# Copies out of PSUM moved from ScalarE to VectorE in an attention and expert kernel

## The chip, the cores and the metric

The kernel runs on one core of one Trainium2 chip. The metric is the device time of one execution in microseconds. Engines are named as in the profile: PE (TensorE), DVE (VectorE), ACT (ScalarE), POOL (GpSimd), SP (SyncE, which issues transfers here).

## What is computed

Local and global attention, and on its output a layer of experts of which each row takes at most one:

```python
scale = 1.0 / np.sqrt(D)                      # batch 8, heads 8, D = 64
s_g = scale * q_g @ concat(k_g, k_l).T        # 32 global queries see all 544 keys
out_g = softmax(s_g) @ concat(v_g, v_l)
s_ll = where(|i - j| <= 32, scale * q_l @ k_l.T, -1e9)   # 512 local queries: a band
a_l = softmax(concat(scale * q_l @ k_g.T, s_ll))         # and the 32 global keys
out_l = a_l @ concat(v_g, v_l)
x = concat(out_g, out_l) as rows              # 8 * 544 = 4352 rows of 512
do = x @ w_skip > 0
e = argmax(x @ w_gate); gate = softmax(x @ w_gate)[e]
out = x, plus for rows with do: gate * (relu(x @ w1[e]) @ w2[e])
```

All in fp32; the experts' products are made of split fp32 parts.

## The kernel before

The attention part goes over 32 pairs of heads (4 pairs in each of 8 batches). The loop at the end of the attention part takes one **unit** u for each pair and is a software pipeline of three: in unit u the pair `cur` (u) gets its scores and exponentials, `prev` (u - 1) its normalization and transposes, `old` (u - 2) its products with the values. Instructions stand on each engine in the order in which this code is written, so the loop's body is the schedule. A pair has 8 blocks of 64 queries, and a block sees 160 keys.

In the order of the body, a unit does this:

- `cur.scores(0)`: PE makes the scores of four blocks (L343); DVE adds the mask and takes the minimum (L355); ACT takes the exponential with its sum (L360).
- `prev.normal(1)`, `prev.scale(1)`: DVE sums and inverts (L385, L386), POOL multiplies (L390). In odd units `prev.normal_g` does the same for the global queries (L420 and L421 on DVE, L422 on POOL).
- `batch_rows(b, k)`: for an earlier batch b, PE turns 128 finished columns of `xT` into rows (L540 into `pr`), ACT copies them out of PSUM (L541) and SP sends them to `out`. With k = 0 come the logits of the batch on PE (L549), which ACT copies (L553), with k = 3 their transposes (L559), which DVE reduces (L560).
- `old.values(0)`, `values(1)`, `values_g`: PE multiplies the probabilities with the values into two PSUM tiles, `pvs[0]` for even blocks of queries and `pvs[1]` for odd ones (L474, L481, L493). ACT copies both into `xT` (L501, two instructions of 128x256). `prev.turn_g(0)`: a stream transpose on DVE (L458).
- `cur.normal(0)`, `cur.scale(0)`, `cur.scores(1)`: as above, for the other half of the pair.
- `old.gather_g(0)`, `gather_g(1)`: DVE adds up the global queries' part of the two tiles (L508, L506). `prev.turn_g(1)`: L458 again.
- `prev.turn(0)`, `turn(1)`: PE transposes the probabilities (L430); DVE copies the first half out of PSUM, ACT the second (L433).
- in odd units `prev.turn_pg`: PE transposes the global probabilities (L442, L443), copied by DVE and ACT (L448, L451). In even units `cur.scores_g`: PE scores of the global queries for two pairs (L405), their minimum on DVE (L409), their exponential on ACT (L414).
- from unit 4, for as long as there are weights of the first expert left: a cast on ACT and a subtraction on POOL (L181, L182), 16 in all.

`batch_rows` runs with k = (u - 6) mod 4 in units 6 to 25 for the batches 0 to 4, so odd k falls into odd units. Batch 3 has a fifth piece, the global rows (L523, in unit 21). The rows of batches 5 and 6 come later in the body, after `gather_g` (`LATE_ROWS`): (5,0) and (5,1) in unit 25, (5,2) in 26, (5,3) in 27, and all four of batch 6 in unit 29. In units 25 and 29 that is the unit in which `old` is the last pair of that batch. Batch 7 goes through `rows` (L523, L528) at the end.

The PSUM tiles of tag "t" (`pr`, `pst`, `psl`, `pl`, `pq`) share three buffers, those of tag "v" (`pv`) two; `xr`, the rows on their way out, has five buffers in SBUF. After the attention part the rows are gathered by expert with indirect transfers, and the experts follow (L827 to L930), PE busy nearly throughout.

Of the kernel before, what the change touches and what calls it, by code (L numbers as in the profile page):

```python
# [28 lines left out]
QB = 64  # L29
# [14 lines left out]
def kernel(  # L44
# [12 lines left out]
    nc = tc.nc  # L57
# [9 lines left out]
    def ps_t(name):  # L67
        return ps.tile([P, 512], F32, tag="t", name=name, bufs=3)
# [117 lines left out]
    with ExitStack() as actx:  # L186
# [130 lines left out]
        def head(h):  # L317
            return slice(h * D, (h + 1) * D)

        def pair(u):  # L320

            b, p = divmod(u, NP)
            q, k, vv = qs[u % NQ], ks[u % NQ], vw[u % NV]
# [129 lines left out]
            pvs = {}  # L453
# [33 lines left out]
            def values_g():  # L487
                for o in range(2):
                    for odd in range(2):
                        pvi = pvs[odd][:, 0:384].rearrange("d (j r) -> d j r", r=96)  # L490
                        for h in range(2):
                            s = head(h ^ odd)
                            nc.tensor.matmul(  # L493
                                pvi[head(h), :, o * SG:(o + 1) * SG], vg[s, p, o, head(h)],
                                pgTs[0][s, odd:NB:2, :], start=False, stop=o == 1,
                                skip_group_check=True,
                            )
                x4 = xT[b][:, p, :].rearrange("d (j a q) -> d a j q", a=2, q=QB)
                for odd in range(2):
                    pvi = pvs[odd][:, 0:384].rearrange("d (j r) -> d j r", r=96)  # L500
                    nc.scalar.copy(x4[:, odd], pvi[:, :, 0:QB])  # L501

            def gather_g(odd):
                pv, xg = pvs[odd], xTg[b // 4][:, p, b % 4, :]
                if odd:
                    nc.vector.tensor_add(xg, xg, pv[:, QB:96])  # L506
                else:
                    nc.vector.reduce_sum(  # L508
                        xg, pv[:, 0:384].rearrange("d (s r) -> d r s", r=96)[:, QB:96, :],
                        axis=AX.X,  # L510
                    )

            return SimpleNamespace(
                scores=scores, normal=normal, scale=scale, scores_g=scores_g,
                normal_g=normal_g, turn=turn, turn_pg=turn_pg, turn_g=turn_g,
                values=values, values_g=values_g, gather_g=gather_g,
            )

        def rows(src, lg, k, dsts, halves, xr):
            for c2 in halves:  # L520
                pr = ps_t("pr")
                for c in range(2):
                    nc.tensor.matmul(  # L523
                        pr[:, c * XW:(c + 1) * XW], src(2 * c2 + c), idw[:, 2 * c2 + c, :],
                        start=True, stop=True,
                    )
                pv = pr[:, 0:2 * XW].rearrange("p (c n) -> p c n", n=XW)
                nc.scalar.copy(  # L528
                    xr[:, c2 * 256:(c2 + 1) * 256].rearrange("p (c n) -> p c n", n=P),
                    pv[:, :, 0:P],  # L530
                )
                nc.vector.tensor_copy(lg[:, k, 2 * c2:2 * c2 + 2, :], pv[:, :, P:XW])
            if halves[-1] == 1:
                for part, r0, n in dsts:
                    nc.sync.dma_start(out[r0:r0 + n, :], xr[part:part + n, :])

        def rows_turn(src, xr, dsts):
            pr = ps_t("pr")
            for c in range(NC):
                nc.tensor.transpose(pr[:, c * P:(c + 1) * P], src(c), ident)  # L540
            nc.scalar.copy(xr, pr)  # L541
            for part, r0, n in dsts:
                nc.sync.dma_start(out[r0:r0 + n, :], xr[part:part + n, :])

        def logits(b):

            pl = ps_t("pl")
            for c in range(NC):
                nc.tensor.matmul(  # L549
                    pl[c * 32:(c + 1) * 32, :], w32[:, c, :], xT[b][:, c, :],  # L550
                    start=True, stop=True,
                )
            nc.scalar.copy(lT, pl)  # L553

        def logits_turn(lg):
            pq = ps_t("pq")
            for t in range(4):
                ts_ = slice(t * P, (t + 1) * P)
                nc.tensor.transpose(pq[:, ts_], lT[:, ts_], ident)  # L559
            stages.insert(0, lambda: nc.vector.reduce_sum(  # L560
                lg[:, 0:4],
                pq.rearrange("p (t c e) -> p t e c", t=4, c=NC)[:, :, 0:E + 1, :],
                axis=AX.X,
            ))
# [75 lines left out]
        lgb, lgs, lgw, xrs = {}, {}, {}, {}  # L640
        LK = 0

        def batch_rows(b, k, halves=(0, 1)):
            T = 5 if b % 4 == 3 else 4
            whole = b < B - 1
            bs = (b,) if b >= B - 2 else (b - b % 2, b - b % 2 + 1)
            t0 = 4 * (b - bs[0])
            if b not in lgs:
                if b == bs[0]:
                    lgw[b] = (  # L650
                        wk.tile([P, 9, E + 1], F32, name="lg2") if len(bs) > 1
                        else rt.tile([P, 5, E + 1], F32, name="lg", bufs=2)
                    )
                lgs[b] = lgw[bs[0]][:, t0:t0 + T]
                if T == 5:
                    lgb[b] = rt.tile([P, 5, NC, E + 1], F32, name="lgb", bufs=1)
            if halves[0] == 0:
                xrs[b, k] = sm.tile([P, DM], F32, name="xr", bufs=5)
            hf = b // 4

            def src(c):
                if k < 4:
                    return xT[b][:, c, k * P:(k + 1) * P]
                return xTg[hf][:, c, :, :].rearrange("d b q -> d (b q)")

            dsts = [(0, b * S + SG + k * P, P)]
            if k == 4:
                dsts = [(bb * 32, (4 * hf + bb) * S, 32) for bb in range(4)]
            if k < 4 and whole:
                rows_turn(src, xrs[b, k], dsts)  # L670
                if k == LK:
                    logits(b)
                if k == 3:
                    logits_turn(lgs[b])
            else:
                rows(src, lgb[b], k, dsts, halves, xrs[b, k])
            if k == T - 1 and halves[-1] == 1:
                if T == 5:
                    ts_ = slice(4 if whole else 0, 5)
                    stages.append(lambda: nc.vector.reduce_sum(  # L680
                        lgs[b][:, ts_], lgb[b][:, ts_].rearrange("p t c e -> p t e c"), axis=AX.X
                    ))
                if b != bs[-1]:
                    return
                T += t0
                steps, send = route(
                    bs, lgw[bs[0]][:, 0:T], T, nc.vector if b >= B - 2 else nc.gpsimd
                )
                stages.extend(steps)
                if b == B - 2:  # L690
                    stages.append(
                        lambda: nc.vector.tensor_scalar_max(base[:, 0:1], base[:, 0:1], float(GRP))
                    )
                stages.append(lambda: sends.extend([lambda t=t: send(t) for t in range(T)]))
# [5 lines left out]
        with tc.manual_schedule(engines=engines):  # L700
# [19 lines left out]
            for u in range(NU + 2):  # L720
# [14 lines left out]
                def late_rows():  # L735
                    for b, k in LATE_ROWS.get(u, ()):
                        batch_rows(b, k)
                    if u == NU - 1:
                        for k in range(5):
                            batch_rows(B - 1, k, (0,))  # L740
# [11 lines left out]
                if 0 <= bp < B - 3:  # L752
                    batch_rows(bp, kp)
                    if kp == 3 and bp % 4 == 3:
                        batch_rows(bp, 4)
# [328 lines left out]
```

## Time and profile before

| | us |
|---|---|
| three runs | 1484.32, 502.81, 506.65 |
| their median | 506.65 |
| the profiled execution | 501.2 |
| its span, first to last instruction | 499.4 |

| engine | busy us | share of the span | instructions |
|---|---|---|---|
| PE | 454.5 | 91% | 4962 |
| DVE | 300.0 | 60% | 1221 |
| ACT | 290.8 | 58% | 883 |
| POOL | 228.2 | 46% | 236 |

The attention part fills about the first 240 us of the span, the experts the rest. A timeline row gives start, duration, engine, line, operation, output<-input, shape and count; in brackets stands the idle time of that engine just before, and what ended it. A count over 1 means that several instructions of the kind are merged into one row. A row of a line's own view gives the shortest, median and longest duration in ns. A row of the waits gives the total in us, the number of waits and the longest.

### The profile page before, as it was taken

The numbers are of one execution on the slowest core, as the hardware profiler recorded it, in microseconds if no ns is written. First come the engines' busy times: TensorE is split into PE (matmuls) and PEld (weight loads), VectorE is DVE, ScalarE is ACT, GpSimd is POOL, SyncE is SP. The second block draws the span as 40 slices with busy tenths as digits, with TensorE's granted clock in tenths as the row PEclk, the third lists the DMA queues.
The fourth block names the chain that finished last, engine by engine and source line by source line (L and its number), as shares of the span: only waits on it lengthen the run. The fifth ranks groups of instructions, "written<-read, shape, count | busy, mean of one in ns | idle before, by whom it ended". The sixth has DMA issues, their size and how long they took to land. (4 is left out here: it accounts for less than half of the span.)

```text
span 499.4 us, 13645 instructions
## 1 busy us (share of the span) xinstructions
PE 454.5 (91%) x4962; PEld 367.2 (74%) x4962; DVE 300.0 (60%) x1221; ACT 290.8 (58%) x883; POOL 228.2 (46%) x236
## 2 busy tenths in 40 slices
PE   8898999999989998888699999999999999999991
PEld 3575676676666776566597979798978989788881
DVE  6886767877657867784344318783923848157210
ACT  5688999899877888765342208481713635245200
POOL 6556666668864667767345015142300431023200
PEclk9999999999999999999799999999999999999997
DMA  8989888888977798720446406975740849203100
GB/s 250 274 294 319 255 278 243 286 281 188 282 207 229 241 190 265 162 65 2 150 170 170 158 24 197 366 235 191 249 153 7 278 174 323 82 26 129 46 15 17
DMA packets 50545, 93.32 MB, mean 187 GB/s; under 512 B 15596, under 2 KB 19948, under 8 KB 50448
## 3 DMA queue, kind: packets, MB, share of 16 engines
q1 hardware_dynamic: 44624, 81.83, 52.5%
q0 software_dynamic: 5824, 10.25, 6.2%
q8 instruction: 55, 0.90, 0.8%
q14 instruction: 42, 0.34, 0.2%
HBM read 82.91 MB, written 14.67 MB: 195 GB/s over the span
## 5 line engine op out<-in xcount | busy, mean ns | idle before, releaser
L360 ACT ACTIVATE prob<-prob,nmx 128x160 f32<-128x160 f32 x256 | 106.4, 418 | 16.4 <-DVE nmx L355 14.9
L390 POOL TENSOR_TENSOR prob<-prob,inv 128x640 f32<-128x640 f32 x64 | 80.1, 1257 | 32.1 <-ACT prob L360 15.4
L853 ACT ACTIVATE hh<-ph 128x256 fp32r<-128x256 f32 x72 | 27.7, 384 | 79.5 <-PE ph L848 74.1
L930 POOL DMA_INDIRECT out_dram<-yo,six x12 | 12.2, 1018 | 130.0 <-DVE yo L929 112.1
L864 PE MATMUL py<-w2h,hh 128*128 128x512 f32 x144 | 57.1, 397 | 0.0
L864 PE MATMUL py<-w2h,hlw 128*128 128x512 f32 x144 | 56.8, 395 | 0.0
L864 PE MATMUL py<-w2l,hh 128*128 128x512 f32 x144 | 56.7, 394 | 0.0
L343 PE MATMUL pss<-ks,qs 64*64 64x160 f32 x1024 | 50.9, 303 | 2.5 <-DVE nmx L355 1.6
L848 PE MATMUL ph<-xh,w1h 128*128 128x256 f32 x288 | 46.6, 284 | 3.7 <-ACT xh L834 1.5
L474 PEld LDWEIGHTS pv<-ptT,vw 128*64 128x64 f32 x1024 | 39.6, 137 | 12.1 <-issue 4.6
L360 ACT ACTIVATION_READ_ACCUMULATOR prob<-prob,nmx 128x1 f32 x256 | 48.3, 189 | 0.0
L343 PEld LDWEIGHTS pss<-ks,qs 64*64 64x64 f32 x1024 | 33.6, 132 | 19.7 <-issue 13.5
L854 DVE SCALAR_TENSOR_TENSOR hlw<-ph,hh 128x256 fp32r<-128x256 f32 x72 | 30.2, 420 | 29.4 <-ACT hh L853 24.1
L474 PE MATMUL pv<-ptT,vw 128*64 128x64 f32 (+1 forms) x1024 | 44.4, 237 | 2.9 <-issue 1.3
L848 PE MATMUL ph<-xh,w1l 128*128 128x256 f32 x288 | 45.5, 280 | 0.0
L848 PE MATMUL ph<-xl,w1h 128*128 128x256 f32 x288 | 45.4, 280 | 0.0
L848 PEld LDWEIGHTS ph<-xh,w1h 128*128 128x128 f32 x288 | 39.5, 192 | 6.6 <-issue 4.3
L430 PE MATMUL pst<-ident,prob 128*128 128x128 f32 x256 | 37.8, 282 | 6.2 <-POOL prob L390 5.0
L631 POOL DMA_INDIRECT lst<-dat,slu x34 | 34.3, 1008 | 19.1 <-DVE cni L949 10.6
L848 PEld LDWEIGHTS ph<-xh,w1l 128*128 128x128 f32 x288 | 39.2, 191 | 0.0
L848 PEld LDWEIGHTS ph<-xl,w1h 128*128 128x128 f32 x288 | 38.9, 190 | 0.0
L182 DVE TENSOR_TENSOR w1l<-raw,w1h 128x1024 fp32r<-128x1024 f32 x28 | 34.1, 1219 | 6.6 <-ACT w1h L181 5.0
(178 smaller groups left out, 939.7 us busy)
## 6 DMA issues: line engine op xcount, KB each, us to landing
raw<-in_w_dram SPq DMA_DIRECT2D x60, 512.0 KB
vw<-in_v_dram SPq DMA_DIRECT2D x32, 512.0 KB
ks<-in_kT_dram SPq DMA_DIRECT2D x32, 400.0 KB
out_dram<-xr SPq DMA_DIRECT2D x32, 256.0 KB
qs<-in_qT_dram SPq DMA_DIRECT2D x31, 256.0 KB
vgs<-in_vgl_dram SPq DMA_DIRECT2D x32, 64.0 KB
raw<-in_w_dram POOLq DMA_DIRECT2D x4, 512.0 KB
lst<-dat,slu POOLq DMA_INDIRECT x34
```

Source lines behind the costliest of these rows:

```text
L182: eng.tensor_sub(lo, raw, hi.bitcast(F32))
L343: nc.tensor.matmul(banks[odd][head(h ^ odd), j * W:(j + 1) * W], q[head(h), w * QB:(w + 1) * QB], window(k[head(h)], w), start=True, stop= ...
L360: nc.scalar.activation(pt[:, i, :], pt[:, i, :], AF.Exp, bias=nmx[:, i:i + 1], scale=-1.0, accum_out=sums[:, i, 0:1],)
L390: nc.gpsimd.tensor_mul(pt[:, sl, :], pt[:, sl, :], inv[:, sl].unsqueeze(2).to_broadcast([P, 4, W]),)
L430: nc.tensor.transpose(pst[:, i * P:(i + 1) * P], pt[:, 4 * hf + i, 0:KW], ident)
L474: nc.tensor.matmul(pv[head(h), j * 96:j * 96 + n], vv[:, w, head(h)], ptT[:, w, h ^ odd, 0:n], start=j == 0, stop=False, skip_group_check= ...
L631: ins = nc.gpsimd.indirect_dma_start(out=lst, out_offset=bass.IndirectOffsetOnAxis(ap=slu[:, t:t + 1], axis=0), in_=dat[:, bs[j], t - 4 * ...
L848: nc.tensor.matmul(ph[:, 0:GRP], hl[a][:, c, f * P:(f + 1) * P], bb[:, c, :], start=i == 0, stop=i == 3 * NC - 1,)
L853: nc.scalar.activation(hh[:, f, :], ph[:, 0:GRP], AF.Relu)
L854: nc.vector.scalar_tensor_tensor(hlw[:, f, :], ph[:, 0:GRP], 0.0, hh[:, f, :].bitcast(F32), ALU.max, ALU.subtract,)
L864: nc.tensor.matmul(py, a[:, f, ts_], hl[bb][:, f, :], start=f == 0 and i == 0, stop=f == NF - 1 and i == 2,)
L930: ins = nc.gpsimd.indirect_dma_start(out=out, out_offset=bass.IndirectOffsetOnAxis(ap=sidx, axis=0), in_=yo, in_offset=None, bounds_check= ...
```

## The change

Two copies go from ACT to DVE. Of the two copies of a pair's output into `xT`, the one of the odd query blocks (`pvs[1]`) is now issued by DVE, in `gather_g(1)`, right after the addition that reads the same PSUM tile; the one of the even blocks stays on ACT in `values_g`. Of the copies of output rows in `rows_turn`, those with odd k are now issued by DVE in place of ACT. Shapes, buffers and transfers stay as they are. That is 32 copies of 128x256 and 14 of 128x512.

```diff
                                 pgTs[0][s, odd:NB:2, :], start=False, stop=o == 1,
                                 skip_group_check=True,
                             )
+                keep(0, nc.scalar.copy)
+
+            def keep(odd, copy):
                 x4 = xT[b][:, p, :].rearrange("d (j a q) -> d a j q", a=2, q=QB)
-                for odd in range(2):
-                    pvi = pvs[odd][:, 0:384].rearrange("d (j r) -> d j r", r=96)
-                    nc.scalar.copy(x4[:, odd], pvi[:, :, 0:QB])
+                pvi = pvs[odd][:, 0:384].rearrange("d (j r) -> d j r", r=96)
+                copy(x4[:, odd], pvi[:, :, 0:QB])
 
             def gather_g(odd):
                 pv, xg = pvs[odd], xTg[b // 4][:, p, b % 4, :]
                 if odd:
                     nc.vector.tensor_add(xg, xg, pv[:, QB:96])
+                    keep(1, nc.vector.tensor_copy)
                 else:
...
-        def rows_turn(src, xr, dsts):
+        def rows_turn(src, xr, dsts, copy):
             pr = ps_t("pr")
             for c in range(NC):
                 nc.tensor.transpose(pr[:, c * P:(c + 1) * P], src(c), ident)
-            nc.scalar.copy(xr, pr)
+            copy(xr, pr)
...
             if k < 4 and whole:
-                rows_turn(src, xrs[b, k], dsts)
+                rows_turn(
+                    src, xrs[b, k], dsts,
+                    nc.vector.tensor_copy if k % 2 else nc.scalar.copy,
+                )
```

The order of instructions on DVE at the end of an even unit, before (from the last part of a minimum to the minimum of the global scores; "ISA" rows are the minima and their accumulators):

```order
L375 ISA nmg 128x1
L508 TENSOR_REDUCE xTg<-pv 128x32
L506 TENSOR_TENSOR xTg<-xTg,pv 128x32
L458 STREAM_TRANSPOSE pgT<-prob 128x128
L433 COPY ptT<-pst 128x8x64
L409 ISA smg_124,nmg<-psg,m_glob,nmg 128x512
L409 ISA nmg 128x1
```

The same place after (line numbers behind the edit have moved by a few):

```order
L375 ISA nmg 128x1
L511 TENSOR_REDUCE xTg<-pv 128x32
L508 TENSOR_TENSOR xTg<-xTg,pv 128x32
L503 COPY xT<-pv 128x4x64
L458 STREAM_TRANSPOSE pgT<-prob 128x128
L433 COPY ptT<-pst 128x8x64
L409 ISA smg_124,nmg<-psg,m_glob,nmg 128x512
L409 ISA nmg 128x1
```

The copy into `xT` (L503) stands between the gathers and the stream transpose, ahead of L433 and L409; in odd units it stands at the same place. On DVE in the first half of an odd unit, from the global normalization on, before:

```order
L420 TENSOR_REDUCE ing<-sumgt_129 128x1
L421 RECIPROCAL ing<-ing 128x1
L458 STREAM_TRANSPOSE pgT<-prob 128x128
L385 TENSOR_REDUCE inv<-sumt_126 128x4
L386 RECIPROCAL inv<-inv 128x4
L355 ISA prob,nmx<-pss,m_even 128x160
```

And after:

```order
L420 TENSOR_REDUCE ing<-sumgt_129 128x1
L421 RECIPROCAL ing<-ing 128x1
L544 COPY xr<-pr 128x512
L458 STREAM_TRANSPOSE pgT<-prob 128x128
L385 TENSOR_REDUCE inv<-sumt_126 128x4
L386 RECIPROCAL inv<-inv 128x4
L355 ISA prob,nmx<-pss,m_even 128x160
```

The row copy (L544) stands ahead of the stream transpose and of `normal(0)` (L385). On PE in unit 25, where batch 5's first rows are turned, with the engines that each instruction waits for, before:

```order
L540 MATMUL pr<-ident,xT 128x128 x3
L540 MATMUL pr<-ident,xT 128x128 [waits Activation_49]
L549 MATMUL pl<-xT,w_107 32x512 [waits DVE_49]
L549 MATMUL pl<-xT,w_107 32x512 x3
L540 MATMUL pr<-ident,xT 128x128 x4
```

And after:

```order
L543 MATMUL pr<-ident,xT 128x128 x3
L543 MATMUL pr<-ident,xT 128x128 [waits DVE_49,Activation_49]
L552 MATMUL pl<-xT,w_107 32x512 [waits PE_49]
L552 MATMUL pl<-xT,w_107 32x512 x3
L543 MATMUL pr<-ident,xT 128x128 [waits PE_49]
```

The order is the same; the fourth transpose, which reads the batch's last pair, now waits for DVE besides ACT.

## The prediction

> **What bounds the kernel now.** The moved copies all lie in the attention part, so I first read the busy times in a stretch of it, then who waited for whom, then the timeline.
>
> The window from 30 to 230 us, in busy us of each engine:
>
> ```profile
> 30.00:230.00 200.00, 181.98 (x3013) 134.07 (x3009) 146.41 (x873) 169.65 (x634) 137.91 (x134) 1.00 0.79 231
> ```
>
> The columns are PE 182.0, PE's weight loads 134.1, DVE 146.4, ACT 169.7 and POOL 137.9 of 200 us; the granted clock is 1.00. By occupancy ACT is fuller than DVE. Whether it is also what the others wait for is not in this row. The longest waits of ACT are:
>
> ```profile
> ACT probg L414 <- DVE nmg L409: 9.2, 12, 1.7
> ```
>
> ACT, the fuller engine, sat 9.2 us in 12 waits before the exponential of the global rows (L414), because DVE had not finished their minimum (L409). Such a wait comes once in two units, so I follow one L409 to the next in the timeline (start us, duration us, engine, line):
>
> ```profile
> 61.73 0.73 DVE L409 CUSTOM_DVE_ANT_0 smg<-psg,m_glob,nmg 128x512 f32<-128x512 f32 x1
> 69.77 1.06 PE L549 MATMUL pl<-xT,w 128*32 128x512 f32 x8
> 75.80 0.73 DVE L409 CUSTOM_DVE_ANT_0 smg<-psg,m_glob,nmg 128x512 f32<-128x512 f32 x1
> 76.58 0.83 ACT L414 ACTIVATE probg<-smg,nmg 128x640 f32<-128x640 f32 x1 [0.61 <-DVE nmg L409]
> 77.41 0.60 ACT L181 CAST w1h<-raw 128x512 fp32r<-128x512 f32 x1
> 78.09 1.27 POOL L182 TENSOR_TENSOR w1l<-raw,w1h 128x512 fp32r<-128x512 f32 x1 [4.48 <-ACT w1h L181]
> 79.32 1.25 POOL L390 TENSOR_TENSOR prob<-prob,inv 128x640 f32<-128x640 f32 x1
> 80.53 1.25 POOL L422 TENSOR_TENSOR probg<-probg,ing 128x640 f32<-128x640 f32 x1
> 81.84 0.66 PE L442 MATMUL psgT<-ident,probg 128*128 128x128 f32 x4 [0.55 <-POOL probg L422]
> 85.68 0.72 PE L343 MATMUL pss<-ks,qs 64*64 64x160 f32 x16
> 86.44 0.33 DVE L355 CUSTOM_DVE_ANT_0 prob<-pss,m_even 128x160 f32<-128x160 f32 x1 [0.49 <-PE pss L343]
> 87.95 0.19 DVE L506 TENSOR_TENSOR xTg<-xTg,pv 128x32 f32<-128x32 f32 x1
> 88.06 0.30 DVE L458 STREAM_TRANSPOSE pgT<-prob 128x128 f32<-128x128 f32 x1
> 88.29 0.65 DVE L433 COPY ptT<-pst 128x512 f32<-128x512 f32 x1
> 88.86 0.73 DVE L409 CUSTOM_DVE_ANT_0 smg<-psg,m_glob,nmg 128x512 f32<-128x512 f32 x1
> ```
>
> This is a closed loop: L409 on DVE (75.80), its exponential and the weight cast on ACT, three products in a row on POOL (the first waited 4.48 us for the cast), PE's transposes of the global rows (0.55 us waiting for POOL), PE without a gap to the scores of the even unit's second half (85.68), and from there DVE's minima, gathers, stream transpose and copy to the next L409. Each step starts as the one before ends. It took 13.06 us (75.80 to 88.86). The one before took 14.07 (61.73 to 75.80) and holds the logits (L549, 1.06 us of PE) besides: 1.01 longer for 1.06 of extra work inside. So what is put into the loop comes out as time. ACT is on it with two instructions, one of them waiting for DVE; neither is moved by the change.
>
> **The change part by part.** *Prices.* The moved copies don't yet run on DVE. Copies of the same shapes out of PSUM do (min/median/max in ns):
>
> ```profile
> L448 DVE COPY ptT<-psgT x16: 405/424/426, 15.2 to 230.9; 128x256 f32<-128x256 f32 x16
> L448 ACT COPY ptT<-psgT x16: 365/372/375, 15.9 to 231.4; 128x256 f32<-128x256 f32 x16
> L433 DVE COPY ptT<-pst x32: 650/653/693, 14.7 to 235.0; 128x512 f32<-128x512 f32 x32
> 82.53 0.42 DVE L448 COPY ptT<-psgT 128x256 f32<-128x256 f32 x1 [0.21 <-PE psgT L442]
> 82.88 0.28 DVE L451 COPY ptT<-psgL 128x128 f32<-128x128 f32 x1
> ```
>
> The block copy (128x256) takes 0.42 us on DVE, but the next instruction starts 0.35 us after it (82.53 to 82.88): 0.35 is its price in a full queue. Below that lies the step of a DVE instruction with half its elements, 0.23 (L458 at 88.06, next at 88.29), above it its whole duration, 0.42; these are the bounds. The row copy (128x512) takes 0.65 and frees its queue after 0.57 (L433 at 88.29, next at 88.86).
>
> *Block copies of even units.* They stand between L506 and L458, in DVE's run-up to L409, where every row follows the last without a gap: 0.35 us on the loop. Loops with the cast inside run from here:
>
> ```profile
> 34.60 0.73 DVE L409 CUSTOM_DVE_ANT_0 smg<-psg,m_glob,nmg 128x512 f32<-128x512 f32 x1
> 130.62 0.73 DVE L409 CUSTOM_DVE_ANT_0 smg<-psg,m_glob,nmg 128x512 f32<-128x512 f32 x1
> ```
>
> Both ends counted that is 8 instances of L409, so 8 x 0.35 = **+2.8** (1.8 to 3.4). After them the cast and its POOL product are gone and PE, DVE and transfers take turns as the last to come; for the six later even units I take half, **+1.0** (0 to 2.1).
>
> *Odd units, DVE and ACT:*
>
> ```profile
> 77.89 0.16 DVE L421 RECIPROCAL ing<-ing 128x1 f32<-128x1 f32 x1
> 79.58 0.56 ACT L541 COPY xr<-pr 128x512 f32<-128x512 f32 x1
> 79.70 0.16 DVE L385 TENSOR_REDUCE inv<-sumt 128x4 f32<-128x8 f32 x1 [1.45 <-ACT prob L360]
> 80.04 0.63 ACT L501 COPY xT<-pv 128x256 f32<-128x256 f32 x2
> ```
>
> The row copy enters DVE's queue after L421, ahead of the 1.45 us in which DVE waits for ACT's exponentials: 0.57 fits, **0**. Behind it stand the stream transpose and L385; without that cover ten such units would pay 5.7 us. SP's output transfer follows it and the loads queued behind come no later. The block copy of the odd unit stands ahead of PE's values but off the loop: **0**. ACT gives up 14 x 0.46 (79.58 to 80.04) and 32 x 0.26 (two copies in 0.63 less one of 0.37), 14.7 us in all. Its exponentials after 80.04 then wait for DVE's minima, which themselves wait for L385, and the loop's ACT steps wait for L409: worth **0** on the loop.
>
> [...]
>
> *Units whose row follows its own copy.* In units 25 and 29 the rows of a batch are transposed in the unit that copies its last pair:
>
> ```profile
> 178.89 0.33 PE L540 MATMUL pr<-ident,xT 128*128 128x128 f32 x1 [0.21 <-ACT xT L501]
> 179.62 0.19 DVE L506 TENSOR_TENSOR xTg<-xTg,pv 128x32 f32<-128x32 f32 x1
> 181.11 1.11 PE L430 MATMUL pst<-ident,prob 128*128 128x128 f32 x8 [0.31 <-ACT xr L541]
> 207.37 0.33 PE L540 MATMUL pr<-ident,xT 128*128 128x128 f32 x1 [0.52 <-ACT xT L501]
> 208.75 0.19 DVE L506 TENSOR_TENSOR xTg<-xTg,pv 128x32 f32<-128x32 f32 x1
> ```
>
> PE's fourth transpose waited for ACT's copy already. On DVE the copy comes behind the minima and both gathers: after L506 at 179.62 plus 0.11 (87.95 to 88.06) plus 0.42 is 180.15, 1.3 us after 178.89. Of that PE gets back a little, since the row copies it waits for next (0.31 at 181.11) are now shared by two engines: **+1.1** (0.3 to 1.6). For unit 29 it is 208.75 + 0.53 = 209.28 against 207.37, 1.9, less some 0.5 (one ACT step) because two of its four row copies leave ACT: **+1.4** (0.5 to 1.9).
>
> ```profile
> 194.62 0.63 PE L430 MATMUL pst<-ident,prob 128*128 128x128 f32 x4 [0.85 <-DVE lg L560]
> 146.76 0.17 DVE L421 RECIPROCAL ing<-ing 128x1 f32<-128x1 f32 x1
> 148.55 0.74 PE L523 MATMUL pr<-idw,xTg 128*128 128x137 f32 x4 [1.83 <-ACT xr L541]
> 238.57 1.68 PE L523 MATMUL pr<-idw,xT 128*128 128x137 f32 x12 [0.30 <-ACT xT L501]
> 242.26 0.63 PE L827 MATMUL xt<-ident,xfirst 128*128 128x128 f32 x4 [1.31 <-DMA xfirst<-out_dram,six]
> ```
>
> In unit 27 the block copy and a row copy (0.35 + 0.57) come ahead of the reduction L560 for which PE waited 0.85: **+0.7** (0.3 to 0.9). In unit 21 PE waited 1.83 us for a row copy on ACT, which ends near 148.5 (PE goes on at 148.55); on DVE, after L421, it ends near 146.93 + 0.35 + 0.65 = 147.9: **-0.6** (-0.9 to 0). At the end PE's last rows (238.57) wait up to 0.65 longer for the block copy; the 1.31 us that PE then waits for the gather at 242.26 hide it: **0** (to 0.65).
>
> Sum: 2.8 + 1.0 + 1.1 + 1.4 + 0.7 - 0.6 = **+6.4 us**, from the bounds +2.0 to +10.6. What follows the attention part starts later by as much. The profiled execution took 501.2 us (span 499.4), so 507.6. The median of the runs shown is 506.65, but of three runs far apart; the other near one is 502.81. I take a base near 502 and predict 508.5.
>
> **The rivals.** *ACT is the bound.* For: 169.7 busy of 200. If all 14.7 us came off the end: 486.5; half would give 494. Against: ACT's waits for DVE on the loop. It decides if L414 stops waiting for L409. Chance 0.10.
>
> *Everything is hidden.* PE is busy 182 of 200, so what DVE adds could vanish under PE. Then only units 21, 25, 27 and 29 count: about 501 to 504. Against: PE's wait in the loop, 0.55 us for POOL. Chance 0.22.
>
> *DVE becomes the bound.* If the row copy is not covered in odd units (0.57 each, 10 units, 5.7 us) and the odd units' block copies reach the minima too (16 x 0.35 = 5.6), it is 507.6 + 11.3 = 519. For: DVE then is at 146 + 32 x 0.35 + 14 x 0.57, about 166 of 200, and routing steps also use its gaps. Against: the 1.45 us wait. It decides where L385 no longer waits for ACT. Chance 0.13.
>
> **How the numbers follow.** My forecast has 0.55. A change of 2% is 10 us, about what a measurement of this kernel can tell from none. The forecast lies within 2%, with a twentieth above; the hidden case is within. Faster by over 2%: most of the first rival, 0.08. Slower: the third and the forecast's upper end, 0.17. The same: 0.75. The range goes from 499 (hidden, with part of the first rival) to 515 (the sum's upper bound on a base near 504).
>
> **What would show it.** Right: L409 to L409 near 13.4 and 14.4 us up to 145 us; L414 waiting longer for L409; ACT's busy time down by about 14 us with no gain; PE's fourth transpose in units 25 and 29 waiting over 1 us for DVE; L385 of odd units still waiting for ACT. Wrong: loops of 13.06 or shorter, which would mean that ACT or PE closes them; or L385 without a wait, which would mean the third rival.

## The result and the profile after

| | before | after |
|---|---|---|
| median of 20 runs, us | 501.69 | 509.05 |
| span of the profiled execution, us | 499.4 | 507.4 |

The ratio of after to before is 1.0142, with a 95% interval of 1.012 to 1.0164. The change costs 1.4%: within 2%, and clear of zero, though the prediction took 2% for about the least that can be told from none. Runs far above the others (1484.32 us before, 531.45 after) are left out of this ratio and of those below.

The engines' line of the page of after:

```profile
PE 456.1 (90%) x4962; PEld 370.2 (73%) x4962; DVE 317.9 (63%) x1267; ACT 277.0 (55%) x837; POOL 227.3 (45%) x236
```

ACT is relieved as meant (290.8 to 277.0 us), DVE takes more than that on (300.0 to 317.9), and the kernel is slower. In the window from 30 to 230 us, ACT has become the emptier of the two; the columns are those of the prediction's first row:

```profile
30.00:230.00 200.00, 177.04 (x2948) 130.76 (x2950) 158.90 (x883) 150.84 (x570) 131.13 (x128) 0.98 0.81 232
```

The prices of the moved copies come from the views of the two lines in after (min/median/max in ns), and the first view also lists who waited for the block copy (total us, number of waits):

```profile
L503 ACT COPY xT<-pv x32: 345/352/372, 20.7 to 248.7; 128x256 f32<-128x256 f32 x32
L503 DVE COPY xT<-pv x32: 417/418/420, 22.7 to 249.6; 128x256 f32<-128x256 f32 x32
  PE pr L543: 4.2, 2
  PE pr L526: 3.7, 2
L544 DVE COPY xr<-pr x14: 652/690/692, 52.3 to 219.6; 128x512 f32<-128x512 f32 x14
```

The closed loop of the prediction, in the timeline of after:

```profile
77.81 0.73 DVE L409 CUSTOM_DVE_ANT_0 smg<-psg,m_glob,nmg 128x512 f32<-128x512 f32 x1
78.59 0.83 ACT L414 ACTIVATE probg<-smg,nmg 128x640 f32<-128x640 f32 x1 [0.87 <-DVE nmg L409]
81.72 0.16 DVE L385 TENSOR_REDUCE inv<-sumt 128x4 f32<-128x8 f32 x1 [0.83 <-ACT prob L360]
89.58 0.29 DVE L511 TENSOR_REDUCE xTg<-pv 128x32 f32<-128x128 f32 x1
89.90 0.19 DVE L508 TENSOR_TENSOR xTg<-xTg,pv 128x32 f32<-128x32 f32 x1
90.01 0.42 DVE L503 COPY xT<-pv 128x256 f32<-128x256 f32 x1
90.34 0.30 DVE L458 STREAM_TRANSPOSE pgT<-prob 128x128 f32<-128x128 f32 x1
90.56 0.65 DVE L433 COPY ptT<-pst 128x512 f32<-128x512 f32 x1
91.14 0.73 DVE L409 CUSTOM_DVE_ANT_0 smg<-psg,m_glob,nmg 128x512 f32<-128x512 f32 x1
```

The loop takes 13.33 us (77.81 to 91.14) where it took 13.06; ACT waits 0.87 us for L409 where it waited 0.61. Both grew by some 0.26. DVE still waits 0.83 us at L385, so the row copy ahead of it is covered.

In later units PE waits for the new copies. Timeline of after, units 25, 27, 29, 31 and 33:

```profile
183.54 0.30 PE L543 MATMUL pr<-ident,xT 128*128 128x128 f32 x1 [1.53 <-DVE xT L503]
199.28 0.63 PE L430 MATMUL pst<-ident,prob 128*128 128x128 f32 x4 [1.82 <-DVE xr L544]
214.48 0.45 PE L543 MATMUL pr<-ident,xT 128*128 128x128 f32 x1 [2.66 <-DVE xT L503]
235.17 3.54 PE L526 MATMUL pr<-idw,xT 128*128 128x137 f32 x14 [2.62 <-DVE xT L503]
250.14 1.88 PE L526 MATMUL pr<-idw,xT 128*128 128x137 f32 x14 [1.07 <-DVE xT L503]
```

To see where the 8.0 us of the spans go, I set the same events of both timelines side by side. Before, where the prediction has no row:

```profile
221.97 0.74 DVE L409 CUSTOM_DVE_ANT_0 smg<-psg,m_glob,nmg 128x512 f32<-128x512 f32 x1
237.87 0.65 ACT L501 COPY xT<-pv 128x256 f32<-128x256 f32 x2 [2.07 <-PE pv L493]
246.70 1.22 PE L848 MATMUL ph<-xh,w1h 128*128 128x256 f32 x4 [0.68 <-ACT xh L834]
```

And after:

```profile
35.86 0.73 DVE L409 CUSTOM_DVE_ANT_0 smg<-psg,m_glob,nmg 128x512 f32<-128x512 f32 x1
134.06 0.73 DVE L409 CUSTOM_DVE_ANT_0 smg<-psg,m_glob,nmg 128x512 f32<-128x512 f32 x1
229.56 0.74 DVE L409 CUSTOM_DVE_ANT_0 smg<-psg,m_glob,nmg 128x512 f32<-128x512 f32 x1
248.67 0.37 ACT L503 COPY xT<-pv 128x256 f32<-128x256 f32 x1 [2.67 <-PE pv L493]
254.13 0.74 PE L854 MATMUL ph<-xh,w1h 128*128 128x256 f32 x4 [0.75 <-ACT xh L840]
```

| from the event before to | before, us | after, us | added |
|---|---|---|---|
| first L409 of the loops with the cast (from the span's start) | 34.60 | 35.86 | +1.26 |
| the eighth (seven loops) | 96.02 | 98.20 | +2.18 |
| the last L409 | 91.35 | 95.50 | +4.15 |
| ACT's last block copy | 15.90 | 19.11 | +3.21 |
| first product of the experts | 8.83 | 5.46 | -3.37 |
| end of the span | 252.7 | 253.3 | +0.6 |

The loops cost 2.2 us, the late units 7.4, and 3.4 come back at the gather: before, PE waited 1.31 and 2.05 us there for gathered rows; after, those rows are already there when PE comes. Of the first 1.26 us, 0.80 come from the two loops before the table's first row (13.61 for 13.35 us and 12.06 for 11.52), and 0.46 lie ahead of the very first L409, which comes anywhere from 9.64 to 10.66 us in the profiles of this study.

The late waits of units 29 and 31 cost more than their length, because the granted clock falls to 0.50 in them and stays low for some 7 us. Windows of after around units 29 and 31 (columns as above; the clock is the number before the last two):

```profile
213.00:214.00 1.00, 0.00 (x0) 0.00 (x0) 0.96 (x9) 1.00 (x5) 1.00 (x2) 0.98 0.42 82
214.00:215.00 1.00, 0.52 (x5) 0.33 (x9) 0.55 (x2) 0.67 (x5) 0.85 (x2) 0.50 0.27 45
221.00:222.00 1.00, 1.00 (x10) 0.84 (x8) 0.79 (x2) 0.38 (x1) 0.00 (x0) 1.00 2.51 125
234.00:235.00 1.00, 0.00 (x0) 0.00 (x0) 0.96 (x8) 1.00 (x6) 0.84 (x2) 0.72 0.00 0
```

PE stands still from 211.8 to 214.48. The clock falls at about 214.0, still inside that wait, and PE then works without a gap at half the clock until 221. The same happens from 234.4 to 241, from unit 31's wait on. Apart from the last 7 us of the span, where the clock is at 0.50 in both kernels, before has such a stretch at the gather alone, also some 7 us long:

```profile
245.00:250.00 5.00, 4.33 (x19) 3.92 (x20) 2.72 (x13) 1.16 (x3) 0.00 (x0) 0.50 0.28 67
```

### The profile page after: what moved, and what is told of

It reads as the page before. It is cut to its first block, busy times and chain, and to the rows that moved or that the text cites. A ratio compares the mean times of both kernels' runs of the same rounds, so it can differ in the third digit from the quotient of the medians.

```text
span 507.4 us, 13622 instructions
## 1 busy us (share of the span) xinstructions
PE 456.1 (90%) x4962; PEld 370.2 (73%) x4962; DVE 317.9 (63%) x1267; ACT 277.0 (55%) x837; POOL 227.3 (45%) x236
## 5 line engine op out<-in xcount | busy, mean ns | idle before, releaser
L360 ACT ACTIVATE prob<-prob,nmx 128x160 f32<-128x160 f32 x256 | 106.3, 416 | 26.5 <-DVE nmx L355 26.3
L360 ACT ACTIVATION_READ_ACCUMULATOR prob<-prob,nmx 128x1 f32 x256 | 47.9, 187 | 0.0
L430 PE MATMUL pst<-ident,prob 128*128 128x128 f32 x256 | 38.9, 287 | 9.8 <-POOL prob L390 7.9
L474 PE MATMUL pv<-ptT,vw 128*64 128x64 f32 (+1 forms) x1024 | 43.1, 237 | 3.1 <-ACT ptT L433 2.4
L430 PEld LDWEIGHTS pst<-ident,prob 128*128 128x128 f32 x256 | 28.6, 145 | 16.8 <-POOL prob L390 13.2
```

What stands on the lines that cost most here:

```text
L360: nc.scalar.activation(pt[:, i, :], pt[:, i, :], AF.Exp, bias=nmx[:, i:i + 1], scale=-1.0, accum_out=sums[:, i, 0:1],)
L430: nc.tensor.transpose(pst[:, i * P:(i + 1) * P], pt[:, 4 * hf + i, 0:KW], ident)
L474: nc.tensor.matmul(pv[head(h), j * 96:j * 96 + n], vv[:, w, head(h)], ptT[:, w, h ^ odd, 0:n], start=j == 0, stop=False, skip_group_check= ...
```

## The experiments

My theory: the cost has two separate parts, block copies of even units on the loop, and block copies of odd units that PE's late row transposes wait for; row copies and ACT's relief are worth nothing. Rivals: DVE's load as a whole costs, or ACT's relief does count. Ratios are to the kernel before, with their 95% intervals.

**One part at a time.** First block copies alone, then row copies alone.

```diff
-                    nc.vector.tensor_copy if k % 2 else nc.scalar.copy,
+                    nc.scalar.copy,
```

> The block copies of the odd query blocks go to DVE as in the change, all row copies stay on ACT. Theory (the block copies cost by their place: about 0.26 us in each loop of two units, and a wait of 1 to 2.7 us where rows are turned in the unit that copies their last pair, units 25, 29, 31 and 33): as slow as the change or a little slower, ratio 1.012 to 1.018, loops of L409 to L409 of 13.3 and 14.3 us. Rival (DVE is simply too full, so the time goes by the DVE time that is added; the blocks are 32 x 0.34 = 11 of 19 us): ratio about 1.008.

Measured: 1.0133 [1.0095, 1.017], as the theory had it. One wait that looked like a row copy's is here as well: in unit 27, with all row copies on ACT, PE waits 1.79 us where it waits 1.82 in the change, now for ACT's copy:

```profile
201.53 0.63 PE L430 MATMUL pst<-ident,prob 128*128 128x128 f32 x4 [1.79 <-ACT xr L544]
```

```diff
-                    keep(1, nc.vector.tensor_copy)      # in gather_g(1)
+                    keep(1, nc.scalar.copy)             # in values_g
```

> The row copies of odd k go to DVE as in the change, all block copies stay on ACT. Theory: the row copies lie in DVE's wait for ACT, ratio 0.997 to 1.002, loops of 13.06 and 14.07 us as before, the wait of PE in unit 21 (1.83 us) about half. Rival (DVE too full; the rows are 14 x 0.57 = 8 of 19 us): ratio about 1.006.

Measured: 0.9988 [0.9961, 1.0014]; loops of 13.07 and 14.06. The row copies do in fact both things that were expected of them in single units, and these cancel. Timeline of the kernel with row copies alone, units 21 and 27:

```profile
147.42 0.74 PE L530 MATMUL pr<-idw,xTg 128*128 128x137 f32 x4 [0.83 <-DVE xr L548]
194.09 0.63 PE L430 MATMUL pst<-ident,prob 128*128 128x128 f32 x4 [2.01 <-DVE xr L548]
```

Unit 21 waits 1.0 us less than the 1.83 before, unit 27 1.2 us more than the 0.85. So, within the intervals, all of the change's cost is in the block copies. Unit 27's wait grows with either kind of copy and not by the sum of both; the cause stays open.

**Block copies of odd and of even units apart.** In each kernel the row copies are back on ACT, and so are the other units' block copies.

```diff
+            on_dve = u % 2 == 1        # the second kernel: u % 2 == 0
...
+                if not on_dve:
+                    keep(1, nc.scalar.copy)
...
-                    keep(1, nc.vector.tensor_copy)
+                    if on_dve:
+                        keep(1, nc.vector.tensor_copy)
```

> Block copies on DVE in odd units only (they hold units 25, 29, 31 and 33), on ACT in even units, all row copies on ACT. Theory: loops stay at 13.06 and 14.07 us, PE's waits for the block copy in units 25, 29, 31 and 33 are all there, so the attention part ends 5 to 8 us later and the ratio is 1.008 to 1.014. Rival (DVE too full): half of the block copies, ratio about 1.004, and every loop a little longer.

Measured: 1.0062 [1.0033, 1.0092]. The loops are those of before (14.06, 13.07; one of 15.00 for 14.42), and PE waits 1.53, 2.51, 2.62 and 1.36 us for the copy in units 25, 29, 31 and 33. The place of the waits is as expected, the ratio lies below the range that I had written. The ratio alone doesn't exclude the rival's 1.004; the unchanged loops do. Where the 3 us of the median lie, this trace doesn't show: it is of the fastest of 12 executions (501.54 us, median 505.20), and from the eighth L409 to the first product of the experts it takes 115.81 us, no longer than the 116.08 before, for all its late waits.

> Block copies on DVE in even units only, on ACT in odd units, all row copies on ACT. Theory: loops of 13.3 and 14.3 us, no wait of PE for a DVE copy in units 25, 29, 31 and 33; 8 x 0.26 plus up to 6 x 0.3, so 2 to 4 us, ratio 1.004 to 1.008. Rival (DVE too full): the same 1.004 as with the odd units. Rival (all of it comes from the loop): ratio 1.012 to 1.016.

Measured: 1.0068 [1.0041, 1.0096]. Loops of 13.32 and 14.32, and none of the late waits for DVE's block copy. The two excesses add up to 1.0130, against 1.0133 for all block copies, each known to within 0.3 to 0.4 points: by the medians the two parts add up to the whole. This trace alone would not show it: the seven loops cost 1.6 us more than before, and the experts' part, 256.5 for 252.7 us, most of the rest.

**The late copies back to ACT.**

```diff
+            on_dve = u not in (23, 27, 29, 31)
```

> As the change, but in units 23, 27, 29 and 31 the odd blocks' copy stays on ACT (pairs 22, 26, 28, 30 of the values), so units 25 and 33 are as in the change only where their own pair is concerned. Theory (two separate costs, the loop's and that of PE waiting for copies that rows read in the same unit): the loops up to 145 us stay at 13.3 and 14.3; the waits of PE for DVE xT disappear in every unit in which the copy is back on ACT (unit 29's 2.66 and unit 31's 2.62), and the time falls from the change's by about 2 to 4 us, a ratio to before of 1.005 to 1.010. Rival (DVE's load as a whole costs, place does not matter): only 4 of 46 copies are back, so the ratio stays at 1.012 or above.

The expectation takes the code's `u` for the unit. It is the pair, whose copy is issued two units later: on ACT are the copies of units 25, 29, 31 and 33, so all those that late rows wait for.

Measured: 1.0078 [1.0042, 1.0115], as the theory had it. Loops of 13.33 and 14.32 as in the change (a first one of 15.88 apart), no wait of PE for DVE's `xT` is left in the late units, and four copies of 46 bring back 0.64 of 1.42 points, nearly half of the cost. From the eighth L409 to the first product of the experts it takes 116.03 us, where the change takes 120.07 and before 116.08.

**The loop's term doubled.**

```diff
                     keep(1, nc.vector.tensor_copy)
+                    if u % 2 == 0:
+                        keep(1, nc.vector.tensor_copy)
```

> The change, with the copy of the odd blocks issued twice in a row on DVE in even units (same source, same target; the output is the same). Theory (the copy in even units lies on the loop with its whole step): loops of 13.66 and 14.65 up to 145 us, 0.33 more than the change's each, and a ratio to before of 1.019 to 1.025. Rival (the change's 0.26 is not the copy's step but a shift in order or a one-off): loops stay at 13.3 and 14.3, ratio 1.014 to 1.017.

Measured: 1.029 [1.0242, 1.0338]; the undisturbed loops take 13.78 and 14.78. Timeline of this kernel ahead of an L409:

```profile
80.40 0.88 DVE L503 COPY xT<-pv 128x256 f32<-128x256 f32 x2
81.19 0.30 DVE L458 STREAM_TRANSPOSE pgT<-prob 128x128 f32<-128x128 f32 x1
```

Two copies take 0.79 us of the queue, 0.46 more than the one's 0.33 (0.88 from the first's start to the second's end, twice 0.42 and a little: they ran one after the other; why, no run shows). The loop grew by 0.46 too. What was put on DVE there lengthened the loop one for one (0.46 us for 0.46); my 0.33 for the second copy was too small, and the ratio came out above my range. The ratio's distance to the change, 1.5% of some 502, is 7.4 us. That 16 x 0.46 over all even units is 7.4 as well is partly chance: in this trace two loops grew by 2 us, and the one from 141.59 on not at all (13.94 us in both).

**The loop's other side: the cast ahead of the global scores.** ACT waits for L409, then makes L414 and the cast, and POOL waits for the cast. Moving the cast ahead of `scores_g` fills ACT's wait.

```diff
+                if u >= 4 and u % 2 == 0:
+                    weights[0].split(nc.gpsimd, 2)
                 if cur and u % 2 == 0:
                     cur.scores_g()
...
                     if u % 2 == 0:
                         weights[0].load()
-                    weights[0].split(nc.gpsimd, 2)
+                    else:
+                        weights[0].split(nc.gpsimd, 2)
```

> The kernel before, with one move: in even units from 4 on the weight cast and its product on POOL (L181, L182) are issued at the start of the unit's last part, ahead of the global scores, so that on ACT the cast stands ahead of the exponential of the global rows. Theory (the loop runs L409, exponential, cast, POOL's three products, PE): the cast then fills ACT's wait for L409, POOL's first product starts before L409 ends, and the loops get shorter than 13.06 and 14.07 by 0.5 to 1.0 us each, 4 to 8 us in all, a ratio of 0.984 to 0.993. Rival (PE closes the loop by its own work, the wait of 0.55 us apart): loops of 12.5 at the least, ratio 0.990 to 0.998. Second rival (the loop does not run through ACT and POOL): loops of 13.06, ratio 1.0.

Measured: 0.9946 [0.9913, 0.9978], faster, but by less than the theory's range. Timeline, one loop of 12.15 us:

```profile
73.76 0.73 DVE L409 CUSTOM_DVE_ANT_0 smg<-psg,m_glob,nmg 128x512 f32<-128x512 f32 x1
73.83 0.62 ACT L181 CAST w1h<-raw 128x512 fp32r<-128x512 f32 x1
74.52 1.28 POOL L182 TENSOR_TENSOR w1l<-raw,w1h 128x512 fp32r<-128x512 f32 x1 [2.63 <-ACT w1h L181]
74.53 0.83 ACT L414 ACTIVATE probg<-smg,nmg 128x640 f32<-128x640 f32 x1
85.91 0.73 DVE L409 CUSTOM_DVE_ANT_0 smg<-psg,m_glob,nmg 128x512 f32<-128x512 f32 x1
```

POOL's product starts 0.76 us behind L409 (73.76 to 74.52) instead of 2.29 (75.80 to 78.09), and L414 no longer waits. The loop did run through ACT and POOL, and 12.15 us lies below the rival's 12.5. In units 16 to 20, though, loops got longer (15.47 and 14.93 for 14.27 and 14.06); the kernel that undoes this part gains more (below).

The same move on the change:

> The change, with the same move of the cast ahead of the global scores. Theory: the loops get shorter than the change's 13.3 and 14.3 by what the same move brings without the change, so that the change itself still costs its 0.26 per loop and its waits before the late rows: ratio to before 0.998 to 1.007. Rival (with POOL's part out of the loop ACT becomes the bound, and the relief of ACT then pays): loops no longer than those of the kernel before with the cast moved, and a ratio lower than its.

Measured: 1.0033 [0.9998, 1.0069], 0.9 points above its partner, where the change without the move costs 1.4. The intervals of these two differences overlap, so that the change costs less here is likely and not certain.

```profile
74.07 0.73 DVE L409 CUSTOM_DVE_ANT_0 smg<-psg,m_glob,nmg 128x512 f32<-128x512 f32 x1
74.85 0.83 ACT L414 ACTIVATE probg<-smg,nmg 128x640 f32<-128x640 f32 x1 [0.35 <-DVE nmg L409]
86.25 0.73 DVE L409 CUSTOM_DVE_ANT_0 smg<-psg,m_glob,nmg 128x512 f32<-128x512 f32 x1
```

This loop takes 12.18 us, no more than the 12.15 without the change. ACT's waits for DVE grew instead: from 30 to 130 us the first of these kernels has ACT waiting 1.4 us for L355 and 0.2 for L409, the second 5.7 and 2.9:

```profile
ACT prob L360 <- DVE nmx L355: 1.4, 6, 0.3
ACT probg L414 <- DVE nmg L409: 0.2, 1, 0.2
...
ACT prob L360 <- DVE nmx L355: 5.7, 12, 0.5
ACT probg L414 <- DVE nmg L409: 2.9, 8, 0.5
```

So with the change ACT has idle time here that it hadn't without it, and the loop got no longer by DVE's added copy. I read this as ACT's relief paying for what DVE takes on, and no more; no run takes the one without the other. The rival is then half right (the loops, not the ratio), and what is left of the change's cost goes with the late waits, which are unchanged (1.53, 2.66, 2.62 us).

Keeping the move to units 4 to 14, where it helps:

```diff
+                if 4 <= u < 16 and u % 2 == 0:
+                    weights[0].split(nc.gpsimd, 2)
...
+                    if u % 2 == 1 or u >= 16:
+                        weights[0].split(nc.gpsimd, 2)
```

> As the kernel before with the cast moved ahead of the global scores, but only in units 4 to 14; from unit 16 on the cast stands where it stood. With the cast moved everywhere the loops of units 16 to 20 got 15.5 and 14.9 us long against 14.3 and 14.1, since POOL's product of the cast now stood ahead of the routing's indirect transfers and these ahead of the scaling. Theory: loops of 12.2 to 13.4 up to unit 16, 14.3 and 14.1 after it, and a ratio of 0.988 to 0.992. Rival (POOL's work comes back later): 0.994 as with the cast moved everywhere.

Measured: 0.9904 [0.9873, 0.9934], as the theory had it, loops of units 16 to 20 at 14.27 and 14.03 again. This beats both kernels: 1.0% faster than before, and 2.3% than the change by the two ratios (0.9904 / 1.0142).

**The clock.** To part the low clock from the waits ahead of it, PE got work to do in them.

```diff
+                if c == NC - 1:                # unit 29, first rows of batch 6: fill = 16
+                    for _ in range(fill):
+                        nc.tensor.transpose(pr[:, c * P:(c + 1) * P], ident, ident)
                 nc.tensor.transpose(pr[:, c * P:(c + 1) * P], src(c), ident)
```

> The change, with PE's two longest waits for DVE's copy filled: in unit 29, ahead of the transpose that waits 2.66 us, and in unit 31, ahead of the one that waits 2.62 us, PE makes 16 transposes of the identity (0.165 us each) into the place that the waiting one then overwrites. They add no result and PE gains no time for its own work. Theory (part of the change's cost is the granted clock, which fell to 0.50 from 214 to 220 and from 234 to 241 us after these waits and not in the kernel before): the clock stays at 1.00 in both places and the time falls by 2 to 5 us, a ratio of 1.004 to 1.010. Rival (the low clock has another cause, or lies beside other waits): the ratio stays at 1.012 to 1.016.

Measured: 1.0164 [1.013, 1.0198]: no gain, and outside both ranges. Timeline, and the window that was at 0.50 in the change:

```profile
212.81 1.91 PE L548 MATMUL pr<-ident 128*128 128x128 f32 x16
215.65 0.30 PE L549 MATMUL pr<-ident,xT 128*128 128x128 f32 x1 [0.92 <-DVE xT L503]
252.32 0.80 PE L861 MATMUL ph<-xh,w1h 128*128 128x256 f32 x4 [0.68 <-ACT xh L847]
...
218.00:219.00 1.00, 1.00 (x10) 0.85 (x9) 0.82 (x2) 0.59 (x1) 0.69 (x2) 1.00 0.25 71
```

The clock stayed at 1.00 after both waits, so the waits were its cause, and the first product of the experts comes 1.8 us earlier than in the change (252.32 for 254.13). Counted from the L409 of unit 28, ahead of both fills (209.74 here, 208.58 in the change), it comes 3.0 us earlier: by these two traces, this is what the half clock behind the two waits had cost. The median granted clock of its runs is 0.987, of the change's 0.981. But from there to the end this kernel takes 256.1 us (span 508.4) instead of 253.3. The clock now falls at the experts' start instead, from 252.9 to 256.3, and later PE shows one wait for its own sequencer that is 1.1 us in the change, and one "issue" wait (nothing that the profile shows) that the change hasn't:

```profile
PE ph L861 <- PEq L1013: 2.0, 1, 2.0
PE ph L861 <- issue: 1.4, 1, 1.4
```

> The kernel before, with PE's waits for the first gather (1.31 and 2.05 us) filled in the same way: 7 and 12 transposes of the identity ahead of the two groups of transposes of the gathered rows. Theory (after these waits the clock was 0.50 from 243 to 250 us, and the experts' first products took 1.05 to 1.22 us instead of 0.63): the clock stays at 1.00 and the time falls by 1.5 to 3 us, a ratio of 0.994 to 0.997. Rival: no difference, 0.999 to 1.001.

Measured: 1.0081 [1.0045, 1.0118], slower than before and outside both ranges. The second group of gathered rows came later (PE goes on at 247.16 instead of 244.94, still waiting for the gather), the clock fell nevertheless (0.50 from 247.3 to 254.1 us), and the experts took 258.2 us instead of 252.7, again with "issue" waits of 0.8 to 1.1 us that the kernel before hasn't.

> The kernel before with what helped put together: the cast ahead of the global scores in units 4 to 14, the one row copy of unit 21 on DVE (the wait of 1.8 us), all other copies on ACT as before, and the waits for the first gather filled with transposes of the identity. Theory (the gains add): 4 to 6 us from the loops, 1 from unit 21, 1.5 to 3 from the clock, a ratio of 0.981 to 0.987. Rival (what comes earlier waits for the gather): 0.988 to 0.992.

Measured: 0.9998 [0.9972, 1.0025], outside both ranges: no gain is left. The loops and unit 21 (0.85 for 1.83 us) are as expected, but the experts take 259.4 us, where the kernel without the fill and without the one row copy takes 252.3. All three kernels with filled waits lose in the experts' part what they gained or more. That part varies without fills too, between 251.5 and 256.9 us in the profiles of this study, so the fills' share in it isn't isolated; but in the experts' part "issue" waits of PE of 0.8 us and more are in these three alone. Why they come, and why the gather lands later in two of the three, stays open.

## Why the prediction was right, and where it was not

The forecast was 508.5 us, the median is 509.05, and the sum of 6.4 us stands against 7.4 by the medians. Point by point:

- **Prices.** 0.42 us and 0.65 were taken for the copies on DVE; they measure 0.418 and 0.69. The block copy's step in a full queue was taken as 0.35 and is 0.33.
- **Block copies of even units, 0.35 each on the loop.** The mechanism is right (even units alone, doubled copy), the size was 0.26 in undisturbed loops. The copy's step is 0.33 (90.01 to 90.34), and 0.07 comes back one instruction earlier: L511 to L508 takes 0.32 us, where L508 to L506 took 0.39 (the last section shows what went with it). Seven loops cost 2.18 against 7 x 0.35 = 2.45, but that this is so close is luck in part: five grew by about 0.25, one by 0.84 since PE also waited 0.76 us for ACT there (15.26 us for 14.42), and one by 0.06. The two loops before 34.60 cost another 0.80 and were not in the sum.
- **Six later even units +1.0, units 25 +1.1, 27 +0.7, 29 +1.4, 21 -0.6.** Together 3.6; between the eighth and the last L409 it is 4.15. Singly: unit 25 waits 1.53 (before 0.21), within its bounds; 27 0.97 more, 29 2.1 more than the 0.52 before and 21 1.0 less, each just outside. In unit 27 PE waited for the row copy and not for the reduction L560. Unit 29 is the one that was too small, and its half clock wasn't in the sum at all.
- **Row copies of the odd units 0.** Right: 0.9988 [0.9961, 1.0014] for all row copies alone.
- **Tail 0, hidden by the wait for the gather.** Wrong in its working, nearly right in its result. I missed that batch 7's first rows in unit 31 also read a copy of that unit: 2.62 us, and the clock behind it. Up to ACT's last block copy the tail was 3.2 us longer, and 3.4 came back at the gather. I had named its first wait, 1.31 us, as cover, and not the second of 2.05. The last rows' own wait grew by 0.77 us (1.07 for 0.30), a little more than the 0.65 that I allowed.
- **ACT's relief 0.** Right as far as the runs go: 13.8 us of it came with a slower kernel, and the row copies alone, which take 14 instructions of 0.56 us off ACT, changed nothing. From 30 to 230 us ACT's waits for DVE ahead of L360 and L414 grew from 16.3 us (7.1 and 9.2) to 29.6 (16.8 and 12.8), so what ACT was relieved of it spent waiting. No run relieved ACT without loading DVE. ACT was the fullest engine beside PE (169.7 of 200 us) and was waited on (4.48 us by POOL for the cast), but its last step ahead of that stood behind DVE (0.61 us of waiting for L409 in that loop). With that wait filled, the change's loop was as short as its partner's (12.18 and 12.15 us), which suggests that there ACT's work counts.
- **Rivals.** "Everything is hidden" falls with the even units alone, "DVE becomes the bound" with the wait of 0.83 us at L385 and the row copies alone. "ACT is the bound" falls with L414, which waits longer for L409 and not less.

So the mechanism of the loop is right, and the number is right by a sum of which the largest terms hold and, in part by luck, by omissions that nearly cancel: the half clock, unit 31 and the first two loops on the one side, the gather on the other.

## What to carry to other kernels

Before an operation is moved to a less busy engine, follow one loop in the timeline: it matters which of the two engines the loop waits for at that place, and in after's loop a copy of 0.33 us on DVE cost 0.26 while 14 us less on ACT brought no gain. Then look for every later reader of the moved result, unit by unit, and not only for the next one: four copies of 46 carried nearly half of the cost. What did pay here was to give the waiting engine its next independent work first (the cast ahead of the exponential, 1.0%).

## What the runs showed of the hardware

- **PE's granted clock fell from 1.00 to 0.50 in or just behind some of its waits, and stayed there for 3.4 or 6.8 us, the end of the span apart.** In after, the low stretches at 214 and 234 us add up to 6.8 us each by their one-us windows, the one at 278 us, behind a wait of 1.98, to 3.4; before's at 243, from the second of two waits (1.31 and 2.05 us) on, to 6.8. The clock fell 2.1 us into the wait of 2.66 and 1.9 us into the one of 2.62; after's waits of 1.53 and 1.82 in units 25 and 27 left it at 1.00. With block copies alone the clock even fell at 42.7 us, behind two waits of 1.43 and 0.56, for 3.4 us, and one loop took 15.88 us; the change has the same two waits without the fall and a loop of 14.31. So a wait cost more than itself here, by its place: 6.8 us at half clock are at most 3.4 us of PE's work, and the kernel with both waits filled gained 3.0 us for the two stretches together. What decides when the clock falls, and for how long, these runs don't show.
- **A semaphore instruction ahead of an addition went with 0.07 us more in DVE's queue, even with ACT's copies done 1.4 us before.** Before, ACT's copy reads the PSUM tile that the addition L506 reads too, and each of the 32 additions has a semaphore instruction of its own ahead of it. After, where DVE makes that copy, only the last two additions have one. The rows are from the lines' views of before and after:

```profile
L506 DVEq EVENT_SEMAPHORE  x32: 21/21/21, 22.1 to 238.6; - x32
L508 DVEq EVENT_SEMAPHORE  x2: 21/21/21, 245.1 to 249.4; - x2
```

  In before's timeline L508 stands 0.39 us ahead of L506 at 87.95:

```profile
87.56 0.29 DVE L508 TENSOR_REDUCE xTg<-pv 128x32 f32<-128x128 f32 x1
```

  ACT's copies of that unit started at 85.91 and were over 1.4 us ahead of the addition. After, the step is 0.32, but 0.39 and 0.40 at the two additions that kept the instruction. With block copies on DVE in odd units alone, or in even units alone, the steps up to 230 us alternate between 0.32 and 0.39 with the units. That is the 0.07 us that came back in each loop.
- **Filling waits brought no gain here.** 19 or 32 added transposes between 213 and 245 us kept the clock up behind two waits of one kernel, and went with "issue" waits of PE of up to 1.7 us in the experts 100 us and more later. The ratios were 1.0164 for the change's 1.0142, 1.0081 for before's 1, and 0.9998 for 0.9904 without the fill and the one row copy.
